# Attention and MoE on one core: the loads of keys and values of batches 2 and 3 move to ScalarE's queue, and the order's places are written out

## The chip, the core and the metric

One core of a Trainium2 chip runs the whole program in one launch. The metric is device time in microseconds (us). Engines are named as in the profile: PE is TensorE's matmuls and PEld its weight loads, DVE is VectorE, ACT is ScalarE, POOL is GpSimd, and SP is SyncE, which computes nothing here and only issues transfers (DMAs). ACT is also able to issue transfers.

## What is computed

```python
B, H, S, D = 4, 8, 576, 64
scores = q @ k.T / sqrt(D)                      # per batch and head, causal
local  = softmax(scores) @ v
q_p    = where(q > 0, q, exp(q) - 1) + 1
mem    = (q_p @ M_prev) / (q_p @ z_prev + 1e-6)
x      = sigmoid(beta) * mem + (1 - sigmoid(beta)) * local   # 2304 rows of 512
h      = x @ w_in                               # 512 to 2048
g      = max(h, 0) + alpha * min(h, 0)
out    = g @ w_out                              # 2048 to 512, 2304 rows
```

All inputs are f32. Most products are done in f16, with each f32 operand split into a high and a low f16 part, so that one product is three matmuls (or two, for the scores).

## The kernel before

**The work.** Each batch has 576 rows: the first 64 rows of all four batches are handled together at the start (batch "Z", shown as 4 in names), and the other 512 in four blocks of 128. A unit is one head with two blocks ([1, 2] or [3, 4]). A unit goes through a chain: score matmuls (`s`, PE); minimum and mask (`E`, `mx`, DVE); exponential (ACT); the memory's part (POOL); the split into high and low part (`P`, ACT then DVE); a transpose by DMA (`PT<-P`, issued by SP); and the value matmuls (`bank`, PE). Of four pairs of heads comes a group of 256 rows; `xn` (ACT, DVE) is turned by another DMA (`x<-xn`, SP), and the group goes through the MoE: `h` matmuls, `r` (ACT, DVE), `gg` (ACT, DVE), `y` matmuls, and the output through `t` (ACT) to memory (SP). The h and y matmuls of a finished group are what PE does while the next units' chains run.

**Batches.** `load_batch` (line 630) loads q, k, v, M_prev and z_prev of one batch into buffers `q`, `kn`, `vn` and `zb`. `kn` and `vn` have one buffer each, so a load waits until the batch before has been split by `build_qk` and `build_v` (`k<-kn` and `v<-vn`, on ACT and DVE). Per batch there are five loads of keys (phases `L2k`, `L3k` for batches 2 and 3) and six of values and M_prev (`L2v`, `L3v`): 22 loads in all for the two batches, 128 KB or 256 KB each in pieces of 256 bytes. All of them go through `load` (line 668), whose one line issues on `Y`, the SP queue. `Y` also issues every transpose, every swap of halves (`qS<-qT`), the loads of weights and the stores. An engine's queue runs strictly in the order written, and an instruction that waits holds up all behind it.

**The order.** The body of the kernel only records operations: each call on V (DVE), A (ACT), G (POOL), T (PE) or Y (SP) goes to `Work.add` (line 282), with the phase as a tag. `Work.price` (line 330) gives a duration to each. `Work.lay` (line 389) is a list scheduler: each engine takes, of what is ready, the operation with the lowest rank, and time advances by the prices. Transfers share one `wire` there. `Work.issue` (line 459) makes the ranks in three rounds from `STAGES` (line 32): a start from the latest time that each operation may have, offsets for phases and engines, and passes of `lay` forward and backward; then it emits all operations by planned start. So a rank is a priority in a plan, and no time on the chip. In the profile all of these operations have line 487 (the emitting line), and they are told apart by tile names.

Of the kernel before, what the change touches and what calls it, by code (L numbers as in the profile page):

```python
# [20 lines left out]
WC = [1, 1, 1, 1, 1, 1, 1, 1, 1, 1, 1, 1, 1, 1, 0, 1]  # L21
XB = 3
# [9 lines left out]
STAGES = [  # L32
    (2, {
        "A0": 10.6, "A:DVE": 50.6, "BK0": 102.5, "BK:ACT": -27.7, "BK:PE": 3.4, "C0": -56.4, "C1": 22.3, "C2": 335.8,
        "C3": -920, "C:ACT": 1096.2, "C:DVE": -3.8, "C:PE": -943.6, "I": -699.2, "I:DVE": 79.2, "I:POOL": 497.7,
        "J:ACT": 470.6, "J:DVE": 108, "J:PE": -179.3, "K": 47.5, "K:POOL": 2.3, "L0K": -713.8, "L0K:DMA": 228.2,
# [6 lines left out]
        "LW:DMA": 605.3, "LZ": 27.3, "LZ:DMA": -1145.9, "Lz": 8.5, "Lz:DMA": -8.6, "N": 87.9, "N:PE": 292.5,  # L43
        "P01": 4, "P03": 3.7, "P11": 777.2, "P13": 823.4, "P21": 168.1, "P23": 236.6, "P31": -675.3, "P33": -247.2,
        "P:ACT": 988.7, "P:DMA": 668.5, "P:DVE": -882.6, "P:PE": -157.8, "S0": 4737.2, "S1": -1253, "S3": -2953.6,
        "S:ACT": -87.5, "S:DVE": 168.1, "V0": -874.8, "V:DVE": 211.2, "V:PE": -90.8, "a0": 5.7, "a1": 46.8,
        "a2": -161.5, "a3": 389.6, "a4": -42.9, "a:ACT": -265.2, "a:DVE": 239.4, "bk0": -173.5, "bk1": 344.8,
        "bk2": 244.5, "bk3": 3.1, "bk:ACT": -687.5, "bk:DMA": 246.9, "bk:DVE": 1380.7, "bk:PE": 100.3, "bv0": -0.7,
# [5 lines left out]
        "o31": 144.8, "o33": 10.1, "o:ACT": -779.8, "o:DMA": 580.1, "o:DVE": -613.6, "o:PE": 33.3, "oZ": 10.8,  # L54
# [5 lines left out]
        "v:DVE": 634.9, "v:PE": 331.4, "x0": -121.5, "x:ACT": 2.1, "x:DVE": 73.7, "y0_10": -412.5, "y0_11": -68.6,  # L60
        "y0_30": 187.3, "y0_31": 1834.4, "y1_10": -18.1, "y1_11": 103.3, "y1_30": -419.6, "y1_31": 103.8,
        "y2_10": 184.2, "y2_11": 220.2, "y2_30": -3073.8, "y2_31": -122.6, "y3_10": 764.1, "y3_11": 98,
        "y3_31": 447.3, "y4_11": -1599.1, "y:ACT": -1231.1, "y:DMA": 642.8, "y:DVE": -750.7, "y:PE": 1282.7,
    }),
# [4 lines left out]
        "C3:PE": -8.9, "C:ACT": 13.2, "C:DVE": 9.3, "C:PE": -17.2, "I": -57.9, "I:POOL": -8.6, "J:ACT": -18.7,  # L69
# [6 lines left out]
        "LW3": -8.7, "LW3:DMA": -22.1, "LW:DMA": -2.8, "LZ:DMA": -42.6, "Lz:DMA": -4.4, "N": 0.9, "N:PE": -13.7,  # L76
# [5 lines left out]
        "P33:DMA": -3.8, "P33:DVE": -7.4, "P33:POOL": -37, "P:ACT": 15, "P:DMA": -20.1, "P:DVE": 8.9, "P:PE": -86.4,  # L82
# [126 lines left out]
        "y:PE": 143.8,  # L209
    }),  # L210
]
WINDOW = 3413.0
RING, SHARE = 1200, 0.95
NEG = -1.0e37
# [35 lines left out]
class Work:  # L250
# [31 lines left out]
    def add(self, kind, engine, name, a, kw):  # L282
# [35 lines left out]
        if kind == "DMA":  # L318
            hold, move, late, packets = hold
        elif kind == "PE":  # L320
            late = ins[0].shape[0] / 128
            x = kw.get("lhsT")
# [1205 lines left out]
```

## Time and profile before

| | before |
|---|---|
| time, median of 3 runs | 563.89 us (560.77 to 564.72) |
| the profiled execution's own time | 563.66 us |
| its span, first to last instruction | 561.9 us |
| mean granted clock of PE | 0.982 of full speed |
| busy: PE, DVE, ACT, POOL | 536.4, 450.9, 376.7, 82.8 us |
| packets on the one hardware DMA queue | 225968, 64.5% of 16 engines' span |

PE counts as busy in 95% of the span. Matmuls are pipelined: a row's duration overlaps the next row's, so the spacing of the rows, and not their duration, is the pace. Idle time of PE is what counts; that of the others counts only where PE waits for them in the end.

### The profile page before, as it was taken

What the parts mean: (1) busy time and instruction counts of PE and PEld (TensorE: products, weight loads), DVE (VectorE), ACT (ScalarE), POOL (GpSimd) and SP (SyncE); (2) the same over time, 40 slices, a digit from 0 to 9 for tenths busy, and PEclk for the clock granted to TensorE, in tenths of its full rate; (3) what the DMA queues carried; (4) which work ended last, traced back from release to release, by engine and by line L of the source; (5) the groups of instructions that cost most, each with busy time, mean ns of one, the idle gap of its engine ahead of it and who ended that gap; (6) DMA issues with size and microseconds to landing.
All of it is one profiled execution on the core that took longest, in us unless ns stands there. A gap on an engine that the chain in (4) does not pass through costs nothing. (4 is left out here: it accounts for less than half of the span.)

```text
span 561.9 us, 11984 instructions
## 1 busy us (share of the span) xinstructions
PE 536.4 (95%) x4421; PEld 353.5 (63%) x4421; DVE 450.9 (80%) x1197; ACT 376.7 (67%) x790; POOL 82.8 (15%) x142
## 2 busy tenths in 40 slices
PE   9749999999999899999998999999999999999997
PEld 3448654556557566658555766578578765866663
DVE  4989999999999799999897999998679974233232
ACT  2568996778998369978785787796579873232222
POOL 3000510031220012221222110431112110000000
PEclk9869999999999999999998999999999999999999
DMA  8998595836359997579999816799446963000000
GB/s 283 239 353 202 155 238 173 244 94 153 89 127 184 214 231 170 101 140 210 194 201 198 175 34 146 160 232 178 58 118 111 167 138 88 12 11 2 37 1 37
DMA packets 226026, 82.84 MB, mean 147 GB/s; under 512 B 216224, under 2 KB 216240, under 8 KB 225968
## 3 DMA queue, kind: packets, MB, share of 16 engines
q1 hardware_dynamic: 225968, 82.09, 64.5%
q8 instruction: 34, 0.56, 0.4%
q14 instruction: 24, 0.20, 0.1%
HBM read 35.66 MB, written 5.77 MB: 74 GB/s over the span
## 5 line engine op out<-in xcount | busy, mean ns | idle before, releaser
L487 PE MATMUL h<-x,R 128*128 128x256 f16 x1536 | 246.7, 273 | 1.9 <-DMA x<-xn 1.4
L487 PE MATMUL y<-R,gg 128*128 128x512 f16 (+1 forms) x832 | 247.0, 399 | 0.8 <-ACT k L487 0.6
L487 PE MATMUL bank<-v,PT 128*128 128x64 f16 x1224 | 182.1, 193 | 5.3 <-DMA PT<-P 4.5
L487 PEld LDWEIGHTS <-R 128*128 128x128 f16 x1536 | 148.6, 98 | 36.9 <-issue 6.5
L487 PEld LDWEIGHTS <-gg 128*128 128x128 f16 x768 | 74.4, 98 | 78.3 <-DVE gg L487 1.8
L487 PEld LDWEIGHTS <-PT 128*128 128x128 f16 x1224 | 114.4, 98 | 13.6 <-DMA PT<-P 6.9
L487 POOL TENSOR_SCALAR E<-q,nrm,sm 128x64 f32<-128x64 f32 x112 | 67.9, 618 | 310.9 <-DVE sm L487 269.8
L487 ACT ACTIVATE E<-E,mx 128x320 f32<-128x320 f32 (+3 forms) x136 | 81.1, 602 | 21.5 <-DVE mx L487 17.4
L487 DVE SCALAR_TENSOR_TENSOR P<-E,mx,P 128x384 f16<-128x384 f32 (+2 forms) x112 | 75.3, 699 | 8.5 <-ACT P L487 8.4
L487 ACT ACTIVATE P<-E,mx 128x384 f16<-128x384 f32 (+2 forms) x112 | 71.0, 675 | 15.8 <-POOL E L487 12.0
L487 DVE SCALAR_TENSOR_TENSOR r<-r,oma,h 128x256 f32<-128x256 f32 x128 | 56.6, 475 | 20.2 <-ACT r L487 20.0
L487 DVE SCALAR_TENSOR_TENSOR gg<-r,gsc,gg 128x512 f16<-128x512 f32 x56 | 41.8, 748 | 36.5 <-ACT gg L487 35.0
L487 ACT ACTIVATE r<-h 128x512 f32<-128x512 f32 x72 | 42.3, 589 | 35.8 <-PE h L487 23.9
L487 ACT ACTIVATE gg<-r,gsc 128x512 f16<-128x512 f32 x56 | 40.1, 717 | 37.4 <-PE y L487 33.4
L487 DVE CUSTOM_DVE_ANT_0 E<-s,mask,pm 128x320 f32<-128x320 f32 (+2 forms) x96 | 56.9, 608 | 7.6 <-PE s L487 7.5
L487 PE MATMUL s<-k,qT 128*128 128x64 f16 (+5 forms) x136 | 37.9, 294 | 1.3 <-DMA k<-k 1.3
L487 PE MATMUL s<-k,qS 128*128 128x192 f16 (+4 forms) x120 | 34.0, 294 | 0.0
L487 PE MATMUL h<-R 128*128 128x256 f32 x128 | 32.7, 383 | 0.0
L487 PEld LDWEIGHTS h<-R 128*128 128x128 f32 x128 | 22.3, 192 | 6.6 <-issue 3.0
L487 ACT ACTIVATION_READ_ACCUMULATOR E<-E,mx 128x1 f32 x124 | 23.5, 189 | 0.0
L487 ACT ACTIVATE xn<-bank,xsc 128x256 f16<-128x256 f32 x28 | 12.9, 462 | 12.3 <-PE bank L487 12.3
L487 DVE SCALAR_TENSOR_TENSOR xn<-bank,xsc,xn 128x256 f16<-128x256 f32 x28 | 13.4, 480 | 9.4 <-ACT xn L487 9.4
(183 smaller groups left out, 636.7 us busy)
## 6 DMA issues: line engine op xcount, KB each, us to landing
q<-in_q_dram SPq DMA_DIRECT2D x16, 256.0 KB, 4.3
vn<-in_v_dram SPq DMA_DIRECT2D x16, 256.0 KB, 5.2
out_dram<-t SPq DMA_DIRECT2D x16, 256.0 KB, 2.4
kn<-in_moe_w_in_dram SPq DMA_DIRECT2D x6, 512.0 KB, 6.7
kn<-in_moe_w_out_dram SPq DMA_DIRECT2D x6, 512.0 KB, 5.3
kn<-in_k_dram SPq DMA_DIRECT2D x12, 256.0 KB, 4.0
qS<-qT SPq DMA_DIRECT2D x24, 128.0 KB, 2.6
R<-in_moe_w_in_dram SPq DMA_DIRECT2D x4, 512.0 KB, 5.6
```

The lines of the kernel that those rows point to most:

```text
L487: fn(*a, **kw)
```

## The change

One line sends a load to another queue by its phase; the planner's prices of transfers are changed, and it gives ACT's transfers a place on the wire; and the three rounds of ranks are replaced by a table `PLAN` that has one rank, in steps of 0.1 us and coded as differences, for each of the 6253 recorded operations. The list scheduler `lay` still turns the ranks into the order. No operation is added or removed, and no tile changes its shape or number of buffers.

```diff
+ASIDE = ('L2k', 'L2v', 'L3k', 'L3v')
...
-STAGES = [
...
+PLAN = {
...
+    "L2k:ACT": "2165 -605 -107 -18 729",
+    "L2q:DMA": "933 -343 326 24 1360",
+    "L2v:ACT": "1679 104 -122 210 -219 290",
+    "L3k:ACT": "2982 -656 51 191 -336",
+    "L3q:DMA": "1701 3 -701 333 -342",
+    "L3v:ACT": "2753 -343 25 341 -99 289",
...
-        if kind == "DMA":
+        if kind == "DMA" or name == "dma_start":
             hold, move, late, packets = hold
...
-                return (800 + 1.75 * kb if kb > 400 else 1130 + 0.6 * kb), 190 + 3.45 * kb, 1655, -1
+                return (800 + 1.75 * kb, 4.1 * kb, 1700, -1) if kb > 400 else (1130 + 0.6 * kb, 3.78 * kb, 1885, -1)
...
-                return 400, (2.75 if self.phase in ("LW0", "LW1") else 4.9) * kb, 2000, packets
+                rate, late = {"LW0": (3.2, 2600), "LW1": (2.7, 2450)}.get(self.phase, (3.55, 2150))
+                return 400, rate * kb, late, packets
             if run >= 512:
-                return 540, max(300, 4.06 * kb), 1800, packets
-            return 620, (273 if kb > 200 else 200) + 4.17 * kb, 2100, packets
+                if o.tensor.name in self.fixed:
+                    return 400, 1.4 * kb, 1950, packets
+                return (560, 5.3 * kb, 1765, packets) if kb < 200 else (530, 4 * kb, 1800, packets)
+            return (600, 4.5 * kb, 2050, packets) if kb > 200 else (620, 6 * kb, 2090, packets)
...
                 free[x] = done = t + hold
+                if x == "ACT" and move and not back:
+                    wire = max(wire, t + 100) + move
+                    done = wire + late
...
-        for passes, bias in STAGES:
...
-            rank = start
+        plan = {}
+        for x, steps in PLAN.items():
+            at, ranks = 0, []
+            for step, _, times in (y.partition("*") for y in steps.split()):
+                for _ in range(int(times or 1)):
+                    at += int(step)
+                    ranks.append(100.0 * at)
+            plan[x] = iter(ranks)
+        start = self.lay(before, after, [next(plan[f"{op[7]}:{op[0]}"]) for op in ops])
...
     def load(o, i, phase):
         work.phase = phase
-        Y.dma_start(out=o, in_=i)
+        (A if phase in ASIDE else Y).dma_start(out=o, in_=i)
```

## Rows read from the trace of the kernel before

**Rows 1.** Busy time by stage (columns: stretch, its length, engines, PEclk, DMA, GB/s).
```profile
core 0: us, PE busy (x) PEld busy (x) DVE busy (x) ACT busy (x) POOL busy (x), PEclk, DMA share, GB/s
...
20.00:60.00 40.00, 29.68 (x239) 23.48 (x240) 37.70 (x114) 29.17 (x79) 0.00 (x0) 0.79 1.05 274
...
180.00:320.00 140.00, 132.26 (x1188) 89.52 (x1185) 127.83 (x351) 102.56 (x221) 25.80 (x44) 0.99 0.91 186
...
540.00:561.90 21.90, 18.11 (x106) 10.06 (x103) 5.31 (x10) 5.42 (x8) 0.00 (x0) 1.00 0.06 24
sum 561.90, PE 536.37 PEld 353.48 DVE 450.91 ACT 376.67 POOL 82.79; mean PE 89.39 PEld 58.91 DVE 75.15 ACT 62.78 POOL 13.80
```

**Rows 2.** Waits of PE, whole execution (us in total, times, longest).
```profile
PE bank L487 <- DMA PT<-P: 4.5, 5, 2.7
PE bank L487 <- DVE stv L487: 3.5, 1, 3.5
```

**Rows 3.** PE's timeline: rows with idle time before them (start, us, operation, releaser).
```profile
185.86 1.36 PE L487 MATMUL h<-x,R 128*128 128x256 f16 x11 [1.21 <-DMA x<-xn]
...
195.26 0.33 PE L487 MATMUL s<-k,qT 128*128 128x192 f16 x2 [0.94 <-DMA k<-k]
...
282.25 0.20 PE L487 MATMUL bank<-v,PT 128*128 128x64 f16 x1 [1.06 <-DMA PT<-P]
...
302.77 0.20 PE L487 MATMUL bank<-v,PT 128*128 128x64 f16 x1 [2.65 <-DMA PT<-P]
```

**Rows 4.** Busy time by stretches of 4 us around the longest gap, columns as in rows 1.
```profile
300.00:304.00 4.00, 1.35 (x15) 0.92 (x14) 1.91 (x4) 1.45 (x3) 1.69 (x2) 1.00 0.71 155
304.00:308.00 4.00, 4.00 (x16) 1.71 (x14) 2.83 (x11) 2.04 (x5) 0.00 (x0) 0.57 0.93 210
```

**Rows 5.** SP's timeline before that gap.
```profile
294.14 2.07 SPq L487 DMA_DIRECT2D kn<-in_k_dram  x2
296.32 5.59 SPq L487 DMA_TRANSPOSE PT<-P  x2
301.97 1.29 SPq L487 DMA_DIRECT2D kn<-in_k_dram  x2
```

**Rows 6.** ACT's timeline at that gap.
```profile
302.83 1.01 ACT L487 ACTIVATE P<-E,mx 128x384 f16<-128x384 f32 x2 [2.40 <-DMA PT<-P]
```

**Rows 7.** Timelines of SP and DVE around the loads of batch 2.
```profile
198.58 4.04 SPq L487 DMA_DIRECT2D vn<-in_v_dram  x4
...
211.30 1.59 SPq L487 DMA_TRANSPOSE PT<-P  x1
...
203.81 1.00 DVE L487 SCALAR_TENSOR_TENSOR P<-E,mx,P 128x384 f16<-128x384 f32 x2
```

**Rows 8.** The 22 moved loads on SP, by tile, 150 to 330 us (ns min/median/max).
```profile
L487 SPq DMA_DIRECT2D kn<-in_k_dram x10: 433/882/2191, 202.7 to 317.8; - x10
...
L487 SPq DMA_DIRECT2D vn<-in_v_dram x10: 530/842/1282, 198.6 to 310.2; - x10
L487 SPq DMA_DIRECT2D vn<-in_M_prev_dram x2: 640/650/659, 208.1 to 305.7; - x2
```

**Rows 9.** Busy time where these loads are issued, columns as in rows 1.
```profile
180.00:220.00 40.00, 37.68 (x273) 24.53 (x270) 37.07 (x99) 25.17 (x48) 4.01 (x8) 1.00 0.95 207
280.00:320.00 40.00, 36.00 (x324) 24.68 (x323) 34.63 (x104) 28.23 (x67) 8.64 (x14) 0.96 1.06 206
```

**Rows 10.** Transposes of P on SP, 216 to 290 and 295 to 303 us (ns min/median/max).
```profile
L487 SPq DMA_TRANSPOSE PT<-P x14: 1309/2082/3990, 219.5 to 289.1; - x14
...
L487 SPq DMA_TRANSPOSE PT<-P x2: 1327/2743/4159, 296.3 to 300.6; - x2
```

**Rows 11.** PE's timeline: the first row, a run of h matmuls, the last run.
```profile
1.18 10.44 PE L487 MATMUL h<-ones 128*128 128x512 f16 x34 [1.18 <-DVE ones L487]
...
431.21 2.46 PE L487 MATMUL h<-x,R 128*128 128x256 f16 x21
...
546.72 11.39 PE L487 MATMUL y<-R,gg 128*128 128x512 f16 x52
```

More of the change, by code (lines that the diff above doesn't have):

```diff
@@ L29 @@
 PN = [1, 1, 1, 1, 1]
-STAGES = [
[L33 to L36, printed above, removed]
[6 rows of a table removed]
[L43 to L48, printed above, removed]
[5 rows of a table removed]
-        "o31": 144.8, "o33": 10.1, "o:ACT": -779.8, "o:DMA": 580.1, "o:DVE": -613.6, "o:PE": 33.3, "oZ": 10.8,
[5 rows of a table removed]
[L60 to L64, printed above, removed]
[4 rows of a table removed]
-        "C3:PE": -8.9, "C:ACT": 13.2, "C:DVE": 9.3, "C:PE": -17.2, "I": -57.9, "I:POOL": -8.6, "J:ACT": -18.7,
[6 rows of a table removed]
-        "LW3": -8.7, "LW3:DMA": -22.1, "LW:DMA": -2.8, "LZ:DMA": -42.6, "Lz:DMA": -4.4, "N": 0.9, "N:PE": -13.7,
[5 rows of a table removed]
-        "P33:DMA": -3.8, "P33:DVE": -7.4, "P33:POOL": -37, "P:ACT": 15, "P:DMA": -20.1, "P:DVE": 8.9, "P:PE": -86.4,
[21 rows of a table removed]
-        "h4_11:PE": -16.7, "h:ACT": 10, "h:DVE": 8.9, "h:PE": -16.3, "n": -27.5, "n:PE": -9.4, "o01": -15,
[5 rows of a table removed]
-        "o33:DVE": 21.3, "o33:PE": -55.2, "o:ACT": -0.5, "o:DMA": -50.1, "o:DVE": 13.1, "o:PE": -18, "oZ": -97,
[4 rows of a table removed]
-        "q:ACT": 39, "q:DVE": 9.7, "r0:ACT": 0.9, "r0:DVE": 9.9, "r:ACT": 35.7, "r:DVE": 13.6, "s01:ACT": -1.2,
[4 rows of a table removed]
-        "s33:ACT": 1.7, "s33:PE": -49.1, "s:ACT": 12.1, "s:DVE": 8.9, "s:PE": -16.3, "sZ": 8.1, "sZ:ACT": 98.3,
[14 rows of a table removed]
-        "y4_11:PE": -16, "y:ACT": 21.9, "y:DMA": 2.5, "y:DVE": 8.4, "y:PE": -16.3,
-    }),
[4 rows of a table removed]
-        "C3:PE": -26.7, "C:ACT": 47.4, "C:DVE": -22.5, "C:PE": 1, "I:DVE": -32.9, "I:POOL": 4.3, "J": 37.8,
[13 rows of a table removed]
-        "P33:DMA": -13.2, "P33:DVE": -9.1, "P:DMA": -3.5, "P:DVE": -22.3, "P:PE": 0.2, "P:POOL": -11, "S0": 2.9,
[27 rows of a table removed]
-        "o33:PE": 65.8, "o:ACT": 7.4, "o:DMA": -10.7, "o:DVE": -24.8, "o:PE": 144.2, "oZ": -53.6, "oZ:ACT": 8.9,
[9 rows of a table removed]
-        "s33:DVE": -8.2, "s33:PE": 41.6, "s:ACT": -5, "s:DVE": -22.3, "s:PE": 143.8, "sZ": -0.9, "sZ:ACT": 37.5,
[15 rows of a table removed]
-        "y:PE": 143.8,
-    }),
-]
@@ L212 @@
+PLAN = {
[423 rows of a table added]
+}
 WINDOW = 3413.0
@@ L335, in price @@
         size = 2 if o.dtype == F16 else 4
-        if kind == "DMA":
+        if kind == "DMA" or name == "dma_start":
             kb = n * o.shape[0] * size / 1024
             if "transpose" in name:
-                return (800 + 1.75 * kb if kb > 400 else 1130 + 0.6 * kb), 190 + 3.45 * kb, 1655, -1
+                return (800 + 1.75 * kb, 4.1 * kb, 1700, -1) if kb > 400 else (1130 + 0.6 * kb, 3.78 * kb, 1885, -1)
             run = min(x.ap[-1][1] * (2 if x.dtype == F16 else 4) for x in (o, ins[0]))
@@ L342, in price @@
             if run < 256:
-                return 500, 0.45 * packets, 1800, packets
+                return 500, 0.45 * packets, 2000, packets
             if run >= 4096:
-                return 400, (2.75 if self.phase in ("LW0", "LW1") else 4.9) * kb, 2000, packets
+                rate, late = {"LW0": (3.2, 2600), "LW1": (2.7, 2450)}.get(self.phase, (3.55, 2150))
+                return 400, rate * kb, late, packets
             if run >= 512:
-                return 540, max(300, 4.06 * kb), 1800, packets
-            return 620, (273 if kb > 200 else 200) + 4.17 * kb, 2100, packets
+                if o.tensor.name in self.fixed:
+                    return 400, 1.4 * kb, 1950, packets
+                return (560, 5.3 * kb, 1765, packets) if kb < 200 else (530, 4 * kb, 1800, packets)
+            return (600, 4.5 * kb, 2050, packets) if kb > 200 else (620, 6 * kb, 2090, packets)
         if kind == "PE":
@@ L465, in issue @@
                 after[d].append((i, lag))
-        late = [0.0] * len(ops)
-        hold = [max(op[5], op[8][0]) for op in ops]
-        pe = 0.0
-        for i in reversed(range(len(ops))):
-            took = ops[i][8][0] + ops[i][8][1] if ops[i][0] == "DMA" else hold[i]
-            late[i] = min([late[f] - lag for f, lag in after[i]], default=0.0) - took
-            if ops[i][6]:
-                late[i] = pe = min(late[i], pe - hold[i])
-        rank = late
-        for passes, bias in STAGES:
-            rank = [x + 1e3 * sum(bias.get(k, 0) for k in dict.fromkeys((
-                op[7], op[7].rstrip("0123456789_") + ":" + op[0], op[7] + ":" + op[0]))) for x, op in zip(rank, ops)]
-            for n in range(passes):
-                if n:
-                    back = self.lay(after, before, [-s - h for s, h in zip(start, hold)], True)
-                    rank = [-s - h for s, h in zip(back, hold)]
-                start = self.lay(before, after, rank)
-            rank = start
+        plan = {}
[7 more added lines that the diff above has]
+        start = self.lay(before, after, [next(plan[f"{op[7]}:{op[0]}"]) for op in ops])
         with tc.manual_schedule():
```

564 rows, old and new, of tables (PLAN, STAGES) are left out of this document.

## The prediction, made before the changed kernel was run

> **What bounds the kernel now.** I read the busy time by stage first. PE is busy for 536.37 of 561.90 us, so 25.53 us are idle [rows 1]. It is the bound: in the middle it always finds h and y matmuls of finished groups to run while the chains of new units go on, and only where those run out does a late chain cost time. DVE comes close (127.83 of 140 us from 180 to 320), ACT does not (102.56) [rows 1]. So an edit is worth what it takes out of, or puts into, PE's 25.53 us, plus what the clock loses after an idle stretch.
>
> The waits of PE tell whom it waited for; their largest line is the transposes of P, 4.5 us in five waits, and one wait of 3.5 us is for a maximum on DVE in the start [rows 2]. PE's timeline places them. The unavoidable ends are 1.18 us ahead of the first matmul and 3.79 us behind the last (561.9 less 546.72 plus 11.39) [rows 11]. From 20 to 60 us 10.32 us are idle, at a mean granted clock of 0.79 [rows 1]. Between 180 and 320 us there are four larger gaps, 1.21, 0.94, 1.06 and 2.65 us, each ended by a transfer that SP had issued [rows 3].
>
> The longest gap is the one that this change speaks to. At 294.14 us SP issues two loads of keys (2.07 us), then two transposes of P (5.59 us), then loads again [rows 5]. PE gets its transposed P at 302.77 [rows 3], and ACT too was held for 2.40 us, because the buffer of P was not free before the transpose had read it [rows 6]. Behind the gap, from 304 to 308 us, the granted clock is 0.57: PE is busy all through, mostly at the lower of its two levels (1.2 GHz), and loses about 4.00 x 0.43 = 1.72 us [rows 4].
>
> **The change part by part.**
>
> *SP loses 22 loads.* The loads of batch 2 stand in front of ready work as well: four loads of values start at 198.58, P of the first units is done at 203.81 plus 1.00, and its transpose is issued at 211.30 [rows 7], 6.5 us late. There PE still had other work, so I give that nothing. In front of the 2.65 us gap the two loads of keys took 2.07 us of SP's time [rows 5], and of the transposes behind them the slower took 4.159 us on the queue, where the median of the 14 before was 2.082 [rows 10]: another 2.08 us. Together 4.15 us, more than the gap, so the gap closes if both go: 2.65 us and the 1.72 us of clock, 4.37 us. The lower end is that only the queue's 2.07 us go, since the loads still move over the same DMA engines, whose mean share from 280 to 320 is 1.06 [rows 9].
>
> By the Trainium skill, page "DMA: Bandwidth & Descriptors", section "Issuing engines are not separate DMA queues", transfers from all issuing engines run on the same 16 DMA engines and interleave, and issuing from several saves only the time on the sequencer. By that the slow transpose stays slow and this part would be 2.07 us; no row here shows a transpose beside loads from a second queue.
>
> *ACT gains 22 issues.* On SP they took a median of 0.882 us (10 of keys), 0.842 (10 of values) and 0.650 (2 of M_prev) [rows 8]: 18.5 us in all, 9.3 for each batch. No row shows ACT issuing a load, so SP's durations stand for it. ACT is busy 25.17 of 40 us from 180 to 220 and 28.23 of 40 from 280 to 320 [rows 9], so 14.83 and 11.77 us are free, more than 9.3 each time, in the stretches in which the buffers come free. That idle time is the cover. If it were gone, what stands behind a load on ACT is late: the exponentials, P's high part, and the relu `r` that frees the two PSUM buffers of h. PE needs some 2.5 us to fill one (21 matmuls in 2.46 us [rows 11]), so a single issue of 0.88 us passes unseen, and three in a row do not. A load also waits on ACT until DVE has read the old buffer; the plan's ranks of these loads are low, so they go as soon as the planner thinks them possible, and a wrong guess stops ACT. Ends: nothing, and all 18.5 us. I take one issue, 0.9 us, since the free time in rows 9 is larger than the need.
>
> *6253 ranks are replaced and prices of transfers changed.* No instruction is added. The order of the engines may move anywhere, and the diff cannot be read as an order without laying it out, so I bound it. Idle time of PE outside the two ends and the gap above is 25.53 - 1.18 - 3.79 - 2.65 = 17.9 us; from 20 to 60 us the clock loses another 40 x 0.21 = 8.4 [rows 1]. The most that an order can win is those 26.3 us; one that lets PE run dry a second time like the start costs 10.3. The gaps of 1.21, 0.94 and 1.06 us [rows 3] are the kind that an order closes; the start is a chain of loads, maxima and conversions, with DVE busy 37.70 of 40 us [rows 1], and gives little. I take a quarter of the 17.9, 4.5 us, a little above the three gaps' 3.2.
>
> **Sum**, against the profiled execution's 563.66 us (its span is 561.9, with 1.76 around it, and the median of the runs is 563.89, so it is an ordinary one): 563.66 - 4.37 + 0.9 - 4.5 = 555.7, so **556 us**.
>
> **The rivals.**
>
> *Hidden or still shared (no change).* The DMA engines remain full, the transposes remain slow, and the order wins as much as it loses. For it: share 1.06 from 280 to 320 [rows 9]; and only one of the four gaps stands behind a moved load. Against it: PE has nothing else to do at 300 us, so each transpose that comes earlier is time won. Only the 2.07 us go, ACT costs 0.9: 563.66 - 2.07 + 0.9 = 562.5.
>
> *ACT becomes the bound (slower).* If two issuing engines cannot describe transfers at the same time, a load on ACT stands until SP's transpose has been issued: half of 2.08 us on average [rows 10], 22 x 1.04 = 22.9 us on top of 18.5. ACT's free 14.83 + 11.77 = 26.6 us [rows 9] then fall short by 14.8, in stretches where PE already runs dry. With the gap closed that is 563.66 - 4.37 + 14.8 = 574.1. It decides from 26.6/22 = 1.2 us for one issue on; the median on SP is 0.88, the longest 2.19 [rows 8]. Against it: PE's filler work takes up some delay elsewhere. The Trainium skill (same page, section "Queues, rings and completion order") says that SP and ACT each own a ring on the 16 DMA engines, not a descriptor generator of their own; that speaks for this case, and no run so far shows it.
>
> *The start opens up (much faster).* The new ranks also order the start. If its 10.32 idle us [rows 1] went instead of the quarter: 563.66 - 4.37 + 0.9 - 10.3 = 549.9. Against it: the load share there is 1.05 and DVE is full [rows 1].
>
> **How the numbers follow.** About 1% (5.6 us) is what a measurement of this kernel can tell from no change; from 558.3 down it is faster, from 569.5 up slower. My forecast (551 to 558) has 0.40, the open start 0.10, no change 0.28, ACT as the bound, or an order that lets PE run dry anew (563.66 + 10.3 = 574.0), 0.22. So faster 0.50, same 0.28, slower 0.22. The likeliest one's own range is 551 to 561 (the lower end has one more quarter of the order's idle time, the upper one the order winning nothing). The range of 8 in 10 runs from 547, below the open start with a little of its clock, to 571, which leaves out the upper half of the slower case and little below.
>
> **What would show it.** Right: in the new profile the loads `kn<-in_k_dram`, `vn<-in_v_dram` of batches 2 and 3 stand on ACT's queue at 0.6 to 0.9 us each; SP's transposes of P near 300 us take about 2 us; no wait of PE for `PT<-P` above 1 us, and a granted clock of 1.00 from 300 to 320; PE's idle time falls from 25.5 to about 17 us. Wrong: transposes of 4 us beside loads from ACT (shared engines); loads on ACT above 1.2 us, with PE waiting for ACT's `r`, `P` or `gg`; or idle time of PE that moves to another stretch instead of going. If the start shows under 6 us idle from 20 to 60, the order won more than I gave it.

## The result, and the profile after

The changed kernel takes 567.43 us (median of 7 runs, 566.82 to 570.35), against 563.89 us before (7 runs, 560.77 to 564.72). The ratio of the times is 1.0084, 95% interval [1.0054, 1.0113]; it goes by the means of the runs, 567.85 and 563.12 us, which lie 4.7 us apart (the medians 3.5). So the changed kernel is slower, inside 1% and beyond what the measurement leaves open; the forecast was 556. The profiled execution took 570.35 us, the longest of its runs and 2.9 us above their median, with a span of 568.6: some of what its rows lose may be its own.

PE is busy for 536.48 us, as before (536.37), so the 6.7 us of longer span are idle time: 32.1 us for 25.5. First the stages; the columns are those of [rows 1], and the emitting line is now 730.

```profile
0.00:20.00 20.00, 16.95 (x70) 7.27 (x70) 11.58 (x15) 5.84 (x11) 4.22 (x13) 1.00 0.90 273
20.00:60.00 40.00, 27.91 (x229) 22.42 (x229) 36.67 (x118) 25.87 (x70) 0.00 (x0) 0.70 0.99 253
60.00:180.00 120.00, 116.03 (x731) 68.03 (x729) 115.34 (x308) 99.61 (x206) 23.25 (x33) 1.00 0.63 156
180.00:320.00 140.00, 132.28 (x1204) 91.04 (x1205) 127.19 (x347) 97.02 (x208) 23.94 (x42) 0.98 0.90 180
```

Those of before that [rows 1] does not have:

```profile
0.00:20.00 20.00, 18.57 (x74) 7.96 (x74) 12.09 (x25) 5.28 (x9) 4.28 (x13) 1.00 0.96 281
...
60.00:180.00 120.00, 118.33 (x783) 71.60 (x782) 116.66 (x306) 99.37 (x202) 23.65 (x33) 1.00 0.61 156
```

The stage from 180 to 320 us, for which the change was priced, has PE at 132.28 us (132.26 before). What is lost is lost elsewhere, most of it ahead of the first moved load (199.63 us): 1.62 us from 0 to 20, 1.77 us from 20 to 60 (and the clock there falls from 0.79 to 0.70), 2.30 us from 60 to 180. Three of PE's larger waits (whole execution; us in total, times, longest) answer to [rows 2]:

```profile
PE bank L730 <- DMA PT<-P: 4.1, 5, 2.0
...
PE h L730 <- DMA q<-in_q_dram: 3.0, 2, 2.7
...
PE y L730 <- ACT gg L730: 2.9, 2, 2.4
```

The wait for transposes of P is nearly as before (4.5 us then), and new ones stand beside it. In PE's timeline, as in [rows 3]:

```profile
21.09 0.66 PE L730 MATMUL h<-ident,q 128*128 128x128 f32 x4 [2.70 <-DMA q<-in_q_dram]
```

```profile
178.52 1.12 PE L730 MATMUL bank<-v,PT 128*128 128x64 f16 x27 [2.02 <-DMA PT<-P]
```

```profile
285.91 0.32 PE L730 MATMUL s<-k,qT 128*128 128x192 f16 x2 [1.66 <-DMA k<-k]
...
300.52 0.39 PE L730 MATMUL y<-R,gg 128*128 128x512 f16 x1 [2.42 <-ACT gg L730]
```

The gap of 2.65 us at 302.77 is gone. In its place are 2.42 us at 300.52, now for ACT's `gg`, and 1.66 us at 285.91 for a transpose of keys. ACT's timeline tells why `gg` is late (ACTq rows are issues on ACT's queue, "issue" is waiting for nothing that the profile shows):

```profile
292.48 3.00 ACTq L730 DMA_DIRECT2D kn<-in_k_dram  x1
...
295.63 3.46 ACTq L730 DMA_DIRECT2D kn<-in_k_dram  x1
...
299.20 0.56 ACT L730 ACTIVATE E<-E,mx 128x320 f32<-128x320 f32 x1 [2.58 <-issue]
...
299.76 0.70 ACT L730 ACTIVATE gg<-r,gsc 128x512 f16<-128x512 f32 x1
```

And SP's at the same time, for comparison with [rows 5]:

```profile
290.33 4.03 SPq L730 DMA_TRANSPOSE PT<-P  x1
294.47 6.14 SPq L730 DMA_TRANSPOSE k<-k  x2
```

Two loads of keys took 3.00 and 3.46 us to issue on ACT, the third and fourth of four in a row, while SP was issuing transposes (one in 4.03 us, then two in 6.14). The ACT instruction behind the last waited 2.58 us, and `gg` stands behind that. A load of batch 2 (3.38 us at 213.75, the third of its series) held ACT for 2.73 us too; PE's waits near it are under 1 us. Of all the loads on ACT, by tile (ns min/median/max), against [rows 8]:

```profile
L730 ACTq DMA_DIRECT2D kn<-in_k_dram x10: 373/972/3460, 212.4 to 301.5; - x10
```

```profile
L730 ACTq DMA_DIRECT2D vn<-in_v_dram x10: 385/770/1807, 199.6 to 318.0; - x10
```

The medians, 0.97 and 0.77 us, are near those on SP (0.88 and 0.84); the longest is not (2.19 on SP).

### The profile page after: what moved, and what is told of

Read it like the earlier page. It is cut to its first block, busy times and chain, and to the rows that moved or that the text cites. A ratio compares the mean times of both kernels' runs of the same rounds, so it can differ in the third digit from the quotient of the medians.

```text
span 568.6 us, 11982 instructions
## 1 busy us (share of the span) xinstructions
PE 536.5 (94%) x4421; PEld 354.8 (62%) x4421; DVE 453.5 (80%) x1197; ACT 374.7 (66%) x790; POOL 81.2 (14%) x142
## 4 chain that ended last, share of the span: by engine, by line
PE 62%; DVE 16%; DMA 10%; ACT 5%; issue 3%; POOL 1%; SPq 1%; ACTq 1%; DVEq 0%; POOLq 0%
PE y L730 25%; PE h L730 24%; PE s L730 6%; DMA PT<-P 5%; PE bank L730 5%; DVE P L730 3%; DVE R L730 3%; DVE E L730 2%; DVE r L730 2%; DMA E<-in_moe_w_in_dram 2%; ACT q L730 1%; DVE gg L730 1%; DMA vn<-in_v_dram 1%; PE s L558 1%; PE bank L558 1%
## 5 line engine op out<-in xcount | busy, mean ns | idle before, releaser
L730 PE MATMUL y<-R,gg 128*128 128x512 f16 (+1 forms) x832 | 243.4, 397 | 2.9 <-ACT gg L730 2.9
L730 PE MATMUL h<-x,R 128*128 128x256 f16 x1536 | 243.6, 275 | 1.5 <-DVE r L730 1.5
L730 PE MATMUL bank<-v,PT 128*128 128x64 f16 x1224 | 177.9, 194 | 4.5 <-DMA PT<-P 4.1
L730 PEld LDWEIGHTS <-PT 128*128 128x128 f16 x1224 | 112.3, 99 | 11.7 <-DMA PT<-P 5.3
L730 POOL TENSOR_SCALAR E<-q,nrm,sm 128x64 f32<-128x64 f32 x112 | 66.4, 605 | 323.6 <-DVE sm L730 225.8
L730 ACT ACTIVATE P<-E,mx 128x640 f16<-128x640 f32 (+3 forms) x112 | 71.3, 674 | 18.7 <-DMA PT<-P 8.3
L730 DVE SCALAR_TENSOR_TENSOR P<-E,mx,P 128x640 f16<-128x640 f32 (+3 forms) x112 | 76.1, 698 | 8.3 <-ACT P L730 7.9
L730 DVE CUSTOM_DVE_ANT_0 E<-s,mask,pm 128x576 f32<-128x576 f32 (+3 forms) x96 | 57.2, 609 | 9.9 <-PE s L730 9.8
L730 ACT ACTIVATE R<-R,wsc 128x1024 f16<-128x1024 f32 x16 | 18.3, 1142 | 9.4 <-DVE R L730 9.1
L730 ACT ACTIVATE t<-y,u 128x512 f32<-128x512 f32 x18 | 12.2, 679 | 12.9 <-PE y L730 12.9
```

Of the source, the lines that this page charges most:

```text
L730: fn(*a, **kw)
```

## The experiments

All ratios are against the kernel before on the same chip, with the 95% interval. In the kernels below the order of emission is written out as a list: `BEFORE` and `AFTER` are the orders in which the two kernels emit the 6253 operations, `AFTER60` is what the new order plans in its first 60 us, and `ASIDE` holds the phases whose loads go to ACT. `merge(...)` and `spread(...)` only name how a list was put together; they are no code of the kernel.

```diff
-            for i in sorted(range(len(ops)), key=lambda i: (start[i], i)):
+            for i in ORDER:
...
-        Y.dma_start(out=o, in_=i)
+        (A if phase in ASIDE else Y).dma_start(out=o, in_=i)
```

### The two parts, one at a time

**The loads alone.**

```diff
+ORDER, ASIDE = BEFORE, ('L2k', 'L2v', 'L3k', 'L3v')
```

> The order of before, instruction by instruction, and only the 22 loads of keys and values of batches 2 and 3 issued on ACT at the places they had in it. Theory 'order': the loss of 3.5 us comes from the new order, in the start and up to 180 us, before the first moved load; then this stays within 2 us of before (563.9). Theory 'queue': the loads on ACT cost it; then this is 3 to 4 us slower than before, with transposes beside the loads slower than on SP alone or ACT late for PE. My own forecast would have been 4 us faster.

Measured: 561.56 us, 0.9989 [0.9972, 1.0006]. No change.

**The order alone.**

```diff
+ORDER, ASIDE = AFTER, ()
```

> The order of after, with the 22 loads put back on SP's queue at the places they have in that order. Theory 'order': as slow as after, 567.4, within 1.5 us. Theory 'queue': back at 563.9. If both parts matter and the loads on ACT help, this is slower than after.

Measured: 565.19 us, 1.0057 [1.0037, 1.0078]. The order carries most of the loss (3.2 of 4.7 us). The interval overlaps that of the whole change, so the 1.5 us left for ACT's queue in this order are likely, and not shown by these two runs alone.

### Which part of the order

**The new order for its first 1726 operations (up to 188 us in its plan), then that of before; and the reverse, with the loads on ACT and on SP.**

```diff
+ORDER, ASIDE = AFTER[:1726] + [i for i in BEFORE if i not in AFTER[:1726]], ()
```

> The order of after for all that it plans ahead of its first moved load (1726 operations), then the order of before for the rest, loads on SP. Theory 'order' with the loss in the first part: 3 to 6 us slower than before, with 12 us idle and a clock near 0.70 from 20 to 60 us as in after. If the loss arises later, within 1 us of before.

```diff
+ORDER = BEFORE[:1777] + [i for i in AFTER if i not in BEFORE[:1777]]
+ASIDE = ('L2k', 'L2v', 'L3k', 'L3v')
```

> The order of before up to the moved loads (1777 operations), then the order of after for the rest, loads on ACT. Theory 'order' with the loss in the first part: 562 to 564, so no slower than before, and 3 us or more faster than after. If the rest of the order or the loads on ACT carry the loss: 566 to 568.

```diff
-ASIDE = ('L2k', 'L2v', 'L3k', 'L3v')
+ASIDE = ()
```

> As the run that takes the order of before up to the moved loads and that of after for the rest (566.5), but with the 22 loads on SP. If runs of loads on ACT's queue hold up what PE needs in that order (ACT held, PE waiting for r and gg): 562 to 564, 2.5 to 4 us faster than with them on ACT. If it is the rest of the order itself: 566 to 567.

Measured: 1.0063 [1.0039, 1.0087] for the first part alone, 1.0077 [1.0050, 1.0104] for the rest with the loads on ACT, 1.0048 [1.0028, 1.0068] for the rest with them on SP. Each part of the new order loses alone, and the two don't add up (0.63 and 0.48% would be 1.1, and the whole is 0.57), perhaps because the second part was laid for the start that goes with it; that is not shown.

**The start by engines.** First only SP's transfers of the first 60 us in the new order, then only the computing engines'.

```diff
+ORDER = merge(BEFORE for PE, ACT, DVE, POOL; AFTER60 for SP)
```

> The order of before, except that SP's queue takes its loads of the first 60 us in the order of after (44 transfers stand in other places: all eight weight loads of the first block ahead of z and q, alpha later). Loads of batches 2 and 3 on SP. If the order of these loads is what makes the start late: 2 to 4 us slower than before, with the waits of PE for q (2 to 3 us) and a lower clock from 20 to 60 us as in after. If the order of the computing engines does it: within 1 us of before.

```diff
+ORDER = merge(AFTER60 for PE, ACT, DVE, POOL; BEFORE for SP)
```

> The counterpart: SP's queue wholly as before, and PE, DVE, ACT and POOL in the order of after for the first 60 us of the plan, then as before. If the loads make the start late: within 1 us of before, or a little slower, since this order was laid for other arrivals. If the computing engines' order does it: 2 to 4 us slower.

Measured: 1.0214 [1.0193, 1.0235] and 1.0036 [1.0020, 1.0052]. The first is no fair test: PE's order of before wants the transposed `alpha` early, the new order of SP loads it late, and PE stands still for it, which neither kernel does:

```profile
PE bank L439 <- DMA xn<-in_moe_alpha_dram: 11.4, 1, 11.4
```

The second is one: PE spends its warm-up matmuls (`h<-ones`) early and is idle for q, and from 20 to 60 us has the busy time and the clock of the changed kernel (27.91, 0.70) without its order of loads:

```profile
20.00:60.00 40.00, 27.53 (x223) 22.14 (x224) 36.69 (x115) 25.88 (x72) 0.00 (x0) 0.70 1.07 278
```

**The first 60 us alone.**

```diff
+ORDER, ASIDE = AFTER[:480] + [i for i in BEFORE if i not in AFTER[:480]], ()
```

> The new order for what it plans in the first 60 us, then the order before; loads on SP's queue. The new order up to 188 us and the order before from there cost 1.0063. If the start carries all of that, this too is 1.005 to 1.007; if the computing engines' order of the first 60 us is all that counts there (1.0036 alone), it is 1.003 to 1.004 and the stretch from 60 to 188 us carries the rest (1.5 us).

Measured: 1.0029 [1.0011, 1.0047]. So the start costs 1.6 us, and the stretch from 60 to 188 us the rest of 1.0063, about 1.9 us, only just more than the two intervals leave open. That is where PE waits at 178.52 in the changed kernel; the kernel with the new order up to 188 us has this wait too (2.27 us at 178.66), and the one with its first 60 us only has none above 0.5 us from 162 to 188.

### What the 22 loads are worth, and where

**Without them.**

```diff
+                if ops[i][7] in ('L2k', 'L2v', 'L3k', 'L3v'):
+                    continue
```

> The order of before without the 22 loads (keys and values of batches 2 and 3 aren't read; the kernel works on those of batch 1 in their place). This is the most that any place for these loads can win. By my prediction's term (the gap at 300 us and the clock behind it) 4 us faster than before or more. By the rival that other chains end the gaps as well: 1 to 2 us faster.

Measured: 558.46 us, 0.9912 [0.9895, 0.9928]. With no such load on any queue the kernel gains 5.3 us; 4.37 for a move to another queue was four fifths of that.

**Only one batch's loads on ACT**, batch 2's in the new order and batch 3's in the order before.

```diff
+ORDER, ASIDE = AFTER, ('L2k', 'L2v')
```

> The new order, batch 2's 11 loads on ScalarE's queue, batch 3's 11 on SP's. All on SP's was 1.0057, all on ScalarE's 1.0084. If the holds at 290 to 300 us (loads of 3.0 and 3.5 us, ScalarE idle 2.6 us) are what ScalarE's queue costs, this is 1.005 to 1.006; if it is batch 2's loads (3.1 and 3.4 us at 200 and 214 us), 1.008; if both, about 1.007.

```diff
+ORDER, ASIDE = BEFORE, ('L3k', 'L3v')
```

> The order before, batch 3's 11 loads on ScalarE's queue, batch 2's 11 on SP's as before. All 22 on ScalarE's was 0.9989. If batch 2's loads cost there the 1.5 to 2.6 us by which ScalarE runs late from 204 to 250 us, and batch 3's win what the prediction gave them (4.37 us), this is 0.992 to 0.996. If the late stretch is made up for by slack in any case, or the win at 300 us depends on it, it is 0.998 to 1.000.

Measured: 1.0049 [1.0033, 1.0065] and 0.9979 [0.9960, 0.9997].

Where the time goes can be followed by ACT's conversion `q<-kn`, which stands once for each batch: the row near 214 us is behind batch 2's loads, that near 326 us behind batch 3's. ACT's timeline of before:

```profile
213.93 2.33 ACT L487 ACTIVATE q<-kn 128x2560 f16<-128x2560 f32 x1
```

```profile
326.33 2.33 ACT L487 ACTIVATE q<-kn 128x2560 f16<-128x2560 f32 x1
```

with all loads on ACT (first experiment):

```profile
199.94 1.64 ACTq L439 DMA_DIRECT2D vn<-in_v_dram  x1
201.62 0.45 ACT L439 ACTIVATE E<-E,mx 128x192 f32<-128x192 f32 x1 [2.28 <-issue]
...
217.87 2.34 ACT L439 ACTIVATE q<-kn 128x2560 f16<-128x2560 f32 x1 [1.42 <-issue]
```

```profile
325.45 2.32 ACT L439 ACTIVATE q<-kn 128x2560 f16<-128x2560 f32 x1
```

with batch 3's only:

```profile
213.69 2.33 ACT L439 ACTIVATE q<-kn 128x2560 f16<-128x2560 f32 x1
```

```profile
322.28 2.33 ACT L439 ACTIVATE q<-kn 128x2560 f16<-128x2560 f32 x1
```

and without any:

```profile
213.25 2.33 ACT L441 ACTIVATE q<-kn 128x2560 f16<-128x2560 f32 x1
```

```profile
322.75 2.33 ACT L441 ACTIVATE q<-kn 128x2560 f16<-128x2560 f32 x1
```

In the order before, batch 3's loads on ACT win 326.33 - 322.28 less the 0.24 us by which that execution was early at batch 2, 3.81 us; without any load it is 3.58 - 0.68 = 2.90. This is near the 4.37 of the sum, and it stands at the gap near 300 us: the clock from 300 to 320 us is 1.00 in both, and PE's wait for a transpose of P is 1.19 us with batch 3's loads on ACT (at 300.40). Without any load it is not gone either:

```profile
300.88 0.20 PE L441 MATMUL bank<-v,PT 128*128 128x64 f16 x1 [1.03 <-DMA PT<-P]
```

But batch 2's loads on ACT cost: a load of values takes 1.64 us, ACT's next exponential waits 2.28, and the conversion comes 3.94 us late, with 1.42 us of waiting just ahead of it. By batch 3's conversion the first experiment is 0.88 us early and no more. In the medians of the runs the split is not told apart (0.9979 and 0.9989, overlapping): these rows are of one execution each.

In the new order it is the other way round. The changed kernel, and the one with only batch 2's loads on ACT:

```profile
225.28 2.32 ACT L730 ACTIVATE q<-kn 128x2560 f16<-128x2560 f32 x1
```

```profile
328.41 2.33 ACT L730 ACTIVATE q<-kn 128x2560 f16<-128x2560 f32 x1
```

```profile
225.12 2.32 ACT L439 ACTIVATE q<-kn 128x2560 f16<-128x2560 f32 x1
```

```profile
325.02 2.33 ACT L439 ACTIVATE q<-kn 128x2560 f16<-128x2560 f32 x1
```

Batch 2's loads are equal in both; batch 3's on ACT cost 328.41 - 325.02 = 3.4 us (both executions are the longest of their runs; by the ratios it is about 2 us). So the holds at 290 to 300 us are, most likely, what ACT's queue costs there, as that expectation's first case had it.

**The loads spread out on ACT.**

```diff
+ORDER, ASIDE = spread(AFTER, 4), ('L2k', 'L2v', 'L3k', 'L3v')
```

> The changed kernel, each of the 22 loads issued no sooner than four of ScalarE's other instructions after the load before it (18 of them are moved back so; the changed kernel issues them in runs of up to three). If it is the runs of loads that hold ScalarE for 2.6 to 2.7 us (217.17 and 299.20 us), these holds go and the ratio falls from 1.0084 by up to the 1.5 us that the loads cost there against SP's queue, to 1.005 to 1.007. If a single load is held as long by SP's transposes, or if the loads come too late for their readers, it stays at 1.007 to 1.011.

Measured: 577.89 us, 1.0247 [1.0218, 1.0275], outside both cases. Loads moved back so far are late for their readers: batch 2's conversion waits 5.17 us for its keys, and PE waits 5.3 us for DVE's `r` (1.5 in the changed kernel). So the time says nothing on what a series of loads holds. The rows do: ACT's loads of keys by tile, then one of them, and what SP issued beside it.

```profile
L440 ACTq DMA_DIRECT2D kn<-in_k_dram x10: 373/374/632, 215.3 to 313.5; - x10
```

```profile
298.01 0.37 ACTq L440 DMA_DIRECT2D kn<-in_k_dram  x1
```

```profile
297.39 5.82 SPq L440 DMA_TRANSPOSE PT<-P  x1
```

Spread out, none of the 22 loads takes over 0.68 us, not even beside a transpose that SP issues for 5.82 us, and ACT's longest "issue" wait among them is 0.72 us. In the changed kernel the first load of a series of three or more takes 0.37 to 0.44 us and the third 1.35 to 3.38. So what holds ACT is the series of loads; a transpose on SP's queue is not enough. It is not needed either: the load of 1.64 us in the first experiment, the third of its series, went out while SP issued nothing (198.47 to 203.93 us). The longest, 3.00 to 3.46 us, were all beside transposes; whether these added to them, no run here shows.

### The idle start and its clock

TensorE's granted clock in the kernel before is 0.50 from 26 to 30 and from 36 to 44 us, behind stretches in which PE was idle. These runs put matmuls of constants, whose output is overwritten, into the idle time.

```diff
+LAST = 94
+FILL = [(119, 11, LAST), (130, 15, 130), (173, 30, 173), (208, 55, 245), (245, 42, 245)]
...
+                for at, n, o in FILL:
+                    if at == i:
+                        for _ in range(n):
+                            T.matmul(ops[o][2][0], lhsT=ones, rhs=ones, start=True, stop=True)
```

Each entry says ahead of which operation, how many matmuls, and whose output they write (`LAST` is a warm-up matmul, which is repeated as it is; the code is shown shortened, without the lines for it and with `ones` for its operands, cut to the size of the output). This list is for the new order, with the loads on ACT, then for its first 60 us followed by the order before, and for the whole new order, both with the loads on SP:

> The changed kernel with extra matmuls of constants, whose output is overwritten, where TensorE stood idle in its first 42 us: eleven more warm-up matmuls (0.24 us each) ahead of the first transpose of q, and some 140 small ones in the gaps at 24.7, 29.5, 36.2 and 41.5 us. If the new order's loss in the start is the granted clock (0.50 from 24 to 46 us after TensorE stood idle at 18 to 21 us), the clock stays at 1.00, the 2 us of matmuls at 42 to 46 us halve, and the ratio goes from 1.0084 to about 1.003 to 1.005. If the loss is the late q, or ends in a chain of VectorE's work, which runs from 28 to 42 us whatever TensorE does, the clock comes back and the time stays at 1.007 to 1.009.

> The new order for what it plans in the first 60 us, then the order before, loads on SP's queue, and the extra matmuls of constants in TensorE's idle start (eleven warm-ups, 142 small ones). Without the extra ones it was 1.0029. If the granted clock is the new start's cost, the stretch from 42 us on begins 2 us earlier and the ratio is 0.997 to 1.000; if VectorE's chain or the late q sets the start, it stays at 1.002 to 1.004.

> The new order throughout, loads on SP's queue, with the same extra matmuls. Without them it was 1.0057; the changed kernel with them, which has the loads on ScalarE's queue, was 1.0128. If the extra matmuls gain their 2 us here (1.001 to 1.003), it is the loads on ScalarE's queue, met 2 us earlier than the order was laid for, that took the gain away. If it is 1.006 or more, the new order itself gives back what the start gains.

Measured: 1.0128 [1.0096, 1.0161], 1.0044 [1.0019, 1.0068], 1.0162 [1.0135, 1.0189]. None gains, and the last is 1% worse than without. In the order before:

```diff
+FILL = [(130, 30, 130), (132, 18, 132), (208, 50, 240), (240, 42, 240)]
```

> The order of the kernel before, the 22 loads on ScalarE's queue (as in the first experiment, 0.9989), and extra small matmuls of constants in the gaps of TensorE's first 40 us: 48 of 64 columns at 22 to 24.5 us, 50 and 42 of 128 columns ahead of the matmuls at 34.3 and 39.4 us. The kernel before runs at a granted clock of 0.50 from 26 to 31 and from 35 to 45 us. If the clock is what the start loses, these stretches run at 1.00, the 4.5 us of matmuls from 39.4 to 44.5 us halve, and the ratio is 0.994 to 0.997; if VectorE's chain holds the start, it stays at 0.998 to 1.000; if the extra matmuls delay those behind them, above 1.000.

> The kernel before with the extra matmuls of constants in TensorE's first 40 us, loads on SP's queue as before. With the loads on ScalarE's queue it was 0.9931. If the filling alone is what gains, this is 0.993 to 0.995; if the move of the loads has a share in it once the start is shorter, 0.996 or more.

> As the run before this one, with the extra matmuls of constants in TensorE's first 40 us (48 of 64 columns and 92 of 128). With all 22 loads on ScalarE's queue and these it was 0.9931, with all on SP's 0.9936. If batch 3's loads win beside the filled start, 0.988 to 0.991; if the gap at 300 us closes by the shift of 2 us alone, 0.993 to 0.994.

Measured: 559.83 us, 0.9931 [0.9906, 0.9956] with all loads on ACT; 559.99 us, 0.9936 [0.9919, 0.9953] with all on SP; 558.16 us, 0.9939 [0.9910, 0.9968] with batch 3's on ACT. All three beat both kernels, by 0.6 to 0.7% against before, and where the loads are issued makes no difference that the intervals (0.2 to 0.3% to each side) would show.

The clock comes back in either order (stages as before, the filled changed kernel and then the filled order of before; 0.70 and 0.79 without):

```profile
20.00:60.00 40.00, 33.42 (x385) 27.80 (x383) 37.72 (x126) 27.77 (x74) 0.00 (x0) 0.96 0.97 267
```

```profile
20.00:60.00 40.00, 35.69 (x387) 29.36 (x387) 38.58 (x128) 29.81 (x84) 0.06 (x1) 0.91 1.06 278
```

In the new order half of the gain is gone by 54 us: PE now waits there for ACT, where it did not without the filling (PE's timeline of the new start, filled). At its first `h<-R` PE is 2.73 us earlier than unfilled (46.53 for 49.26 us), at this row 1.33 (54.16 for 55.49).

```profile
54.16 0.39 PE L450 MATMUL bank<-wsq,ones 128*128 128x4 f32 x2 [1.32 <-ACT E L450]
```

And a shift of about 2 us at the entry to the stage with the loads changes what that stage takes by more than the shift. The conversions again, first the order before, filled, with its loads on SP:

```profile
212.19 2.34 ACT L450 ACTIVATE q<-kn 128x2560 f16<-128x2560 f32 x1
```

```profile
321.77 2.32 ACT L450 ACTIVATE q<-kn 128x2560 f16<-128x2560 f32 x1
```

then the new start without filling, and with it:

```profile
217.54 2.34 ACT L439 ACTIVATE q<-kn 128x2560 f16<-128x2560 f32 x1
```

```profile
327.05 2.33 ACT L439 ACTIVATE q<-kn 128x2560 f16<-128x2560 f32 x1
```

```profile
215.45 2.34 ACT L450 ACTIVATE q<-kn 128x2560 f16<-128x2560 f32 x1
```

```profile
329.62 2.32 ACT L450 ACTIVATE q<-kn 128x2560 f16<-128x2560 f32 x1
```

Behind the start all three have the order of before on every engine. The first comes 1.74 us earlier than before to batch 2's conversion and 4.56 earlier to batch 3's, with no load moved off SP's queue. PE's wait near 300 us shrank to 1.29 us, and the one in the new start without filling is 1.37; the clock behind both is 1.00.

```profile
298.71 0.20 PE L450 MATMUL bank<-v,PT 128*128 128x64 f16 x1 [1.29 <-DVE gg L450]
```

```profile
304.27 0.20 PE L439 MATMUL bank<-v,PT 128*128 128x64 f16 x1 [1.37 <-DMA PT<-P]
```

From one conversion to the other these two take 109.58 and 109.51 us, as long as the kernel without any of the loads (322.75 - 213.25 = 109.50), where before takes 326.33 - 213.93 = 112.40. The kernel with the new order up to 188 us takes 109.34, and the two with one part of the new start 112.54 and 112.55, with waits of 1.95 and 2.73 us near 300 and a lower clock behind them as before. But for the one without them, all have the loads on SP, and all have the order of before in this stage: the gap that the prediction priced is there in some and not in others, in one execution each.

The last comes 2.09 us earlier than the one without filling, and then 2.57 us later: PE's waits for `x<-xn` between 180 and 340 us are 3.9 us against 1.1. It may hang on which transfer meets which transpose; no run here traced one such meeting back to the start, and that stays open.

## Why the prediction was wrong, point by point

**PE is the bound, and an edit is worth what it takes out of its idle time.** Right: busy time moved by 0.1 us, and idle time by 6.6 of the span's 6.7.

**The gap at 300 us, 4.37 us.** For the profiled execution of the kernel before the size was near: 3.81 us with batch 3's loads on ACT and 2.90 without the loads, in one execution each, though the gap did not close (1.03 us stay without any load). The step that failed is that this was set down as the whole kernel's gain from the change. With all loads on ACT the stage lost at batch 2's loads most of what it won, and over many executions the move won 0.6 us (first experiment), no more than the measurement leaves open. That a gap seen in one profiled execution stands in all was assumed: three kernels with the loads on SP and the order of before in this stage show 1.29 to 1.42 us there at a full clock, and are as quick through it as with no load at all.

**Only the queue's part goes, because the 16 DMA engines are shared.** This was the lower end. Issues of P's transposes on SP, 285 to 325 us (ns min/median/max): before, changed, and without any of the loads.

```profile
L487 SPq DMA_TRANSPOSE PT<-P x8: 1316/1630/4159, 283.8 to 323.5; - x8
```

```profile
L730 SPq DMA_TRANSPOSE PT<-P x7: 1317/1627/5050, 286.8 to 318.4; - x7
```

```profile
L441 SPq DMA_TRANSPOSE PT<-P x8: 1311/1894/3740, 283.6 to 319.9; - x8
```

Loads from ACT do not make transposes short (5.05 us at the longest), which agrees with the Trainium skill, page "DMA: Bandwidth & Descriptors", section "Issuing engines are not separate DMA queues". But with no load at all there is still one of 3.74 us, and the median is no shorter; [rows 10] had one of 3.99 us, in a stretch in which none of the 22 loads is issued. So the 2.08 us that I put down to loads ahead of the slow transpose were mostly not theirs; where the gap shrank, the larger share was more likely the queue's 2.07 us and what followed from it, which no run here shows by itself.

**ACT's issues, 0.9 us.** Mis-sized. The cover, 14.83 and 11.77 us of free time on ACT, was there as a sum and not where it was needed: a load of 3.46 us held ACT 2.58 us and PE 2.42 behind it. The prediction had said that three issues in a row do not pass unseen, and then priced one; the loads went out in series of up to four, and the later ones of a series took far longer than the first. In the order before, batch 2's loads held ACT 2.28 us and made the conversion 3.94 us late; in the new order batch 3's cost 3.4 us between two profiled executions, and about 2 us in the ratios (1.0084 against 1.0049, whose intervals overlap).

**The rival that ACT becomes the bound, 574.1.** That ACT holds PE was right; why, and how much, was not. It had each load stand until SP's transpose has been issued. But beside the transpose of 4.03 us two loads went out in 1.38 us (at 290.85 us), beside the one of 5.82 us a load took 0.37, and the long ones were those late in a series of loads. The Trainium skill (same page, section "Queues, rings and completion order") says that SP and ACT have no descriptor generator of their own. That a load waits for SP's transpose, as the rival drew from it, these rows do not bear out. Half a transpose for each of the 22 was too much, and a few long ones at a full place were enough.

**The new ranks, a gain of 4.5 us.** This is the step that decided, and its sign was wrong: the order alone costs 3.2 us (1.0057), so 7.7 of the 12.7 us between the forecast's 8.0 us of gain and the 4.7 of loss lie here. I took "the most an order can win" as its range and gave a quarter of it, with no row that spoke for a gain; a loss was only in a rival. What happened is near the rival "an order that lets PE run dry anew", though smaller: PE waits 2.70 us for q at 21.09, because the new order spends all 66 warm-up matmuls ahead of it, the clock then stays at 0.70 from 20 to 60, and at 178.52 a wait of 2.02 us for a transpose of P stands where before there was none above 0.21 (160 to 185 us; the 1.21 us at 185.86 of [rows 3] are gone in turn).

**The start "gives little".** Wrong for the order before. Of the 8.4 us that I put down to the clock, the filling won 2.35 us directly (batch 1's conversion of keys comes at 130.20 us for 132.55) and 0.64% in all, 3.6 us, more than any move of the loads did. In the new order 1.33 us of it were left at 54 us, and none at the end.

**The rival "no change", 562.5.** Its time is that of the loads alone (561.56), not for the reason it gave: it had 2.07 us won and 0.9 lost, and the rows show 3.94 lost up to batch 2's conversion and 4.82 won behind it. It was wrong for the whole change, since the order did not win as much as it lost.

## What to carry to other kernels

Price the two halves of a mixed change apart, and give a replaced order a range of both signs: here a new order cost 3.2 us, and filling the idle start moved the kernel by 3.6 us down in one order and 5.9 up in another. Before a gap of one profiled execution is priced, look whether it stands in others. Free time on an engine that is to issue transfers counts only where the transfers come: look at how many go out in a row, and at what stands right behind them. Where TensorE's idle start leaves a low granted clock, matmuls of constants in the gaps can be worth more than moving any transfer, or nothing: they won 0.6% in one order and none in the other.

## What the runs showed of the hardware

A load of keys, 0.37 us on ACT's queue at the shortest, took up to 3.46 us as the fourth of a series of loads, and ACT's own instruction behind it waited 2.58 us; with the loads spread out none took over 0.68 us, also beside a transpose that SP issued for 5.82 us. TensorE's granted clock stayed at 0.50 (1.2 GHz) in the changed kernel from 24 to 46 us, also through stretches that matmuls filled; PE had been idle for most of 18 to 22 us. Rows by 2 us, columns as in [rows 1]:

```profile
18.00:20.00 2.00, 0.40 (x4) 0.15 (x2) 1.97 (x3) 2.00 (x6) 0.00 (x0) 1.00 0.85 184
20.00:22.00 2.00, 0.91 (x6) 0.69 (x7) 1.99 (x4) 1.18 (x2) 0.00 (x0) 1.00 0.62 146
...
26.00:28.00 2.00, 2.00 (x24) 1.57 (x20) 1.09 (x9) 0.53 (x3) 0.00 (x0) 0.50 1.35 198
42.00:44.00 2.00, 2.00 (x11) 2.00 (x10) 2.00 (x5) 0.00 (x0) 0.00 (x0) 0.50 1.16 237
```

With the idle time filled the mean from 20 to 60 us was 0.96 (0.70 without).
